# Attention by heads in small tiles, and the splitting's middle word in PSUM

## The chip, the cores and the metric

The kernel runs on one core of a Trainium2 chip, as one program. The metric is the device time of an execution in microseconds (us), lower is better. The core has five engines with queues of their own: TensorE (PE; its weight loads are shown apart as PEld), VectorE (DVE), ScalarE (ACT), GpSimd (POOL) and SyncE (SP, which issues most transfers). Each engine works through its own queue in the order in which the program wrote it.

## The reference

Three layers follow one another, all in float32 (two weight matrices come in float64):

```python
kv = einsum('bhsd,bhse->bhde', k, v)            # 8 batches, 8 heads, 576 tokens, 64 wide
out = einsum('bhsd,bhde->bhse', q, kv)
x = out / sqrt(mean(out*out, -1) + 1e-6) * g_norm      # per head; then 4608 tokens x 512
h = x @ w_in                                    # 512 -> 2048, float64 weights
x = (maximum(h, 0) + alpha * minimum(h, 0)) @ w_out    # 2048 -> 512
logits = x @ w_gate + modality_bias[modality_id]       # 8 experts, the best one per token
out = gate * (maximum(x @ w1[e], 0) @ w2[e])    # 512 -> 1024 -> 512, each token by its expert
```

## The kernel before

The 4608 tokens go through attention and the dense layer in 12 chunks of 384 tokens, each three tiles of 128. A chunk has 16 steps, one per block of 128 of the 2048 hidden columns. In step s, `first(c, s)` makes the hidden block from `xhi` and `xlo` (x split in two for precision), 12 matmuls that move 384 columns. DVE makes `gg` from it (the bent line with alpha), ACT rounds it to `ghi`, POOL makes the rest `glo`, and one step later `second(c, s - 1)` adds to the three outputs with 9 matmuls that move 512 columns. After the twelve chunks the tokens, scattered by expert into DRAM, are gathered in tiles of 128 and go through their experts (`layer1`, `layer2`).

What the next chunk needs is woven into the steps of the present one. `load_kv` and `kv_mm` bring in a new batch's k and v (seven of the twelve chunks have one) and multiply them, in one pair of heads per step, steps 2 to 5; the last block of 64 rows is a matmul of its own height. `kv_evict` (step 6) writes the two 64 x 64 products of each pair onto the diagonal of `kvbd`, whose other corners stay zero. `attend` (steps 9, 10, 11, one tile each) multiplies q with that block diagonal, four pairs of heads with 128 x 128 weights each. Where a tile lies in two batches, its halves are matmuls of their own, with 64 columns of weights. ACT copies the result to `x` and squares it, DVE sums the squares (`squares`), takes the root in thirteen small steps (`rsqrt`, step 12) and scales (`scale_x`, steps 13 and 14). At step 15 `turn_x` turns x with twelve PE transposes through PSUM, and `take_x` makes `xhi` (ACT) and `xlo` (DVE) from PSUM with the norm's factor `g_sb`.

The router of the chunk before is woven in too: DVE's `dots` (steps 1 to 8), `choose` (step 8: the one-hot `hb`), `count` (two small PE matmuls on `hb`) and `weigh` (step 9), `place` (step 10) and three indirect scatters on POOL (steps 10 to 12). Except in four steps, a piece of the experts' weights is split and stored ahead (`pre_load`, `pre_hi`, `pre_lo`, `pre_store`).

Chunk 0 also splits the float64 weights, 32 halves of 128 x 512, two or more per step (`cut`). Of the two words of a float64 number ACT takes the high one (`cut_a`), and DVE makes a middle word in three instructions: `low_bits` (L163), `sign_bit` (L168), and `high_bits` (L173), which shifts the high word and joins it with the middle one. `cut_c` rounds on ACT (L181) and subtracts on POOL (L182). The middle word `cut_b` lives in SBUF, in two buffers of the later `wg_sb`.

PSUM has eight banks: three for the outputs of `second`, two for `first`, three for all else (`other`). The order of all work is written out by hand (`manual_schedule`); the program's order on each engine is the order of execution.

Of the kernel before, what the change touches and what calls it, by code (L numbers as in the profile page):

```python
# [11 lines left out]
I32 = mybir.dt.int32  # L12
# [32 lines left out]
def fused(ctx: ExitStack, tc, qT, kv, g2, wmoe, alpha, wgate, bias, modality, w12, out):  # L45
# [14 lines left out]
    ps_h = phase1.enter_context(tc.tile_pool(name="ps_h", bufs=2, space=PSUM))  # L60
    ps_a = phase1.enter_context(tc.tile_pool(name="ps_a", bufs=3, space=PSUM))
    pools = []
# [7 lines left out]
    nalpha = one.tile([128, NFB], F32, name="nalpha")  # L70
    g_sb = one.tile([128, 1], F32, name="g_sb")
    pad = one.tile([128, ROW], F32, name="pad")
# [8 lines left out]
    base = one.tile([128, E], F32, name="base")  # L81
    kvbd = [one.tile([128, 4, 128], F32, name=f"kvbd{i}") for i in range(2)]
    xhi = one.tile([128, 4, CT], F32R, name="xhi")
    xlo = one.tile([128, 4, CT], F32R, name="xlo")
# [10 lines left out]
    lg_t, kvps, hot_t, tps_t, pos_t, sq_t, rsqrt_t, yb_t = {}, {}, {}, {}, {}, {}, {}, {}  # L95
    ops = []

# [16 lines left out]
    def load_kv(b, p):  # L114
        if b == 0 and p >= 2:
            o = (p - 2) * 1280
            t = scratch[:, o:o + 1280].rearrange("p (s c) -> p s c", c=256)
        else:
            t = two.tile([128, 5, 256], F32, tag="kv", name="kv")
# [37 lines left out]
    def cut_b(n):  # L157
        o = 3072 + (n % 2) * 512
        return scratch[:, o:o + 512].bitcast(I32)

    def low_bits(n):
        if n < 2 * NFB:
            V.tensor_scalar(cut_b(n).unsqueeze(2), raw_t[n][:, :, 0:1].bitcast(U32), 2.0 ** -29, 7.0, ALU.mult, ALU.min)  # L163
# [20 lines left out]
    def cut(later=None, between=None):  # L184
        h = n_cut[0]
        n_cut[0] += 1
        cut_c(h)
        steps = [lambda: sign_bit(h + 1), lambda: low_bits(h + 2), lambda: high_bits(h + 1)]
        if later is None:
            for step in steps:  # L190
                step()
        else:
            later.extend(steps)
        if between:
            between()
        cut_a(h + 2)
        load_w(h + 7)
# [21 lines left out]
    def kv_mm(b, p):  # L219
        if p == 0:  # L220
            kvps[b] = four(other())
        t = kv_t.pop((b, p))
        for s in range(5):
            n = 128 if s < 4 else 64
            PE.matmul(kvps[b][:, p, :], t[0:n, s, 0:128], t[0:n, s, 128:256], start=(s == 0), stop=(s == 4))

# [4 lines left out]

    def attend(c, t):
        bank4 = other()
        ps = four(bank4)
        tok = c * CT + t * 128
        b0, b1 = tok // S, (tok + 127) // S
        q = q_t[c]
        for p in range(4):
            if b0 == b1:
                PE.matmul(ps[:, p, :], q[:, p, t * 128:(t + 1) * 128], kvbd[b0 % 2][:, p, :], start=True, stop=True)  # L240
            else:
                for i, b in enumerate((b0, b1)):
                    o = t * 128 + i * 64
                    PE.matmul(ps[i * 64:i * 64 + 64, p, :], q[:, p, o:o + 64], kvbd[b % 2][:, p, :], start=True, stop=True)
        x = three.tile([128, 8, 64], F32, tag="x", name="x")
        xt_t[c, t] = x
        flat = bank4
        A.copy(x.rearrange("p a b -> p (a b)"), flat)
        A.activation(junk, flat, AF.Square)

# [62 lines left out]
    def scale_x(c, t):  # L313
        x = xt_t[c, t]
        src = ops[t].rearrange("p a (h b) -> p (a h) b", b=64) if c == 0 and t < 2 else x
        r = ms_t[c][:, t * 8:t * 8 + 8].unsqueeze(2).to_broadcast([128, 8, 64])
        (G if c == 0 and t == 2 else V).tensor_tensor(x, src, r, ALU.mult)

    def turn_x(c, k):
        if k == 3:  # L320
            ps = bank(CT)
        else:
            ps = other(CT)
        for t in range(3):
            x = xt_t[c, t].rearrange("p a b -> p (a b)")
            PE.transpose(ps[:, t * 128:(t + 1) * 128], x[:, k * 128:(k + 1) * 128], ident)
        tps_t[k] = ps

    def take_x(k):
        ps = tps_t.pop(k)  # L330
        A.activation(xhi[:, k, :], ps, AF.Identity, scale=g_sb)
        V.scalar_tensor_tensor(xlo[:, k, :], ps, g_sb, xhi[:, k, :].bitcast(F32), ALU.mult, ALU.subtract)  # L332

# [98 lines left out]
    def count(c):  # L432
        hot, hb, lg = hot_t[c]
        ps = other(48).rearrange("p (n a b) -> p n a b", n=2, a=3)
# [142 lines left out]
    def load_rows(i):  # L577
# [5 lines left out]
        r = G.value_load(tab, min_val=0, max_val=E * BUCKET + 1024 - 128)  # L583
        rows[i] = three.tile([128, 4, 128], F32, tag="x", name="rows")
        src = xb[ds(r, 128)]
# [81 lines left out]
    def turn_h(i):  # L667
        h = hh.pop(i)
        hi = two.tile([128, 2, 512], F32R, tag="kv", name="hth")
        lo = two.tile([128, 2, 512], F32R, tag="raw", name="htl", bufs=3)  # L670
# [63 lines left out]
    with tc.manual_schedule():  # L734
# [13 lines left out]
        for i in range(2):  # L748
            V.memset(kvbd[i], 0.0)
        V.memset(magic, 0x5F3759DF)  # L750


# [7 lines left out]
        warm(WARM[0])  # L760
        ops.extend(four(other()) for _ in range(3))
        ms_t[0] = one.tile([128, 24], F32, tag="ms", name="ms")
        for t in range(3):
            xt_t[0, t] = three.tile([128, 8, 64], F32, tag="x", name="x")
        for p in range(5):
# [16 lines left out]
        for t in range(3):  # L782
            sum_half(t, 1)
        A.copy(xt_t[0, 2].rearrange("p a b -> p (a b)"), ops[2].rearrange("p a b -> p (a b)"))
        for n in range(3, 6):
# [10 lines left out]
        for k in range(4):  # L796
            turn_x(0, k)
            take_x(k)
        high_bits(1)
        V.tensor_scalar(nalpha, alpha_sb, -1.0, None, ALU.mult)  # L800
        cut_a(2)
        low_bits(2)
        load_w(6)
# [7 lines left out]
        for c in range(NCH):  # L811
# [3 lines left out]
            for s in range(NFB):  # L815
                edge = s == NFB - 1
                if edge and nxt < NCH:
                    for k in range(2):
                        turn_x(nxt, k)
                between = None  # L820
                if edge and nxt < NCH:
                    between = lambda: [take_x(k) for k in range(2)]
                elif s == 0 and c > 0:
                    between = lambda: [second(c - 1, NFB - 1, (2,)), y_out(c - 1, 1)]
# [16 lines left out]
                if edge and nxt < NCH:  # L841
                    for k in range(2, 4):
                        turn_x(nxt, k)
                        take_x(k)
                    second(c, s, (0, 1))
                elif edge:
                    turn_rows(0)
                    second(c, s)

                if kvb and s < 4:  # L850
                    load_kv(kvb[0], s)
                if kvb and 2 <= s < 6:
                    kv_mm(kvb[0], s - 2)
                if kvb and s == 6:
                    kv_evict(kvb[0])
                if nxt < NCH:
# [3 lines left out]
                    if at <= s < at + 3:  # L860
                        attend(nxt, s - at)
                    if s == 11 and nxt + 1 < NCH:
# [5 lines left out]
                    if s == 13:  # L868
                        scale_x(nxt, 0)
                        scale_x(nxt, 1)  # L870
                    if s == 14:
                        scale_x(nxt, 2)

                if c > 0:
# [13 lines left out]
                    if nxt < NCH and 10 <= s < 13:  # L888
                        scatter(c - 1, [s - 10])
                    if nxt == NCH and s == 10:  # L890
# [27 lines left out]
        pools.append(ctx.enter_context(tc.tile_pool(name="ps_p", bufs=2, space=PSUM)))  # L918
        pools.append(ctx.enter_context(tc.tile_pool(name="ps_o", bufs=1, space=PSUM)))

        add = lambda *js: [far_add(c, j) for j in js]
# [95 lines left out]
```

## Time and profile before

| | us |
|---|---|
| median of 3 runs | 1484.96 (1483.78 to 1485.65) |
| profiled execution | 1483.74 |
| its span | 1482.1 |
| PE busy | 1410.6 (95%) |
| PE weight loads busy | 1207.5 (81%) |
| DVE busy | 1077.2 (73%) |
| POOL busy | 704.3 (48%) |
| ACT busy | 526.0 (35%) |

The span runs from the first to the last instruction. Matmuls are pipelined: a matmul's duration is its way through the array, and the next one starts before it ends. What one costs is read from start to start. An fp32 matmul shows as two passes, a split one (fp32r) as one. The mean granted clock of PE is 0.989 of 2.4 GHz.

### The profile page before, as it was taken

The numbers are of one execution on the slowest core, as the hardware profiler recorded it, in microseconds if no ns is written. First come the engines' busy times: TensorE is split into PE (matmuls) and PEld (weight loads), VectorE is DVE, ScalarE is ACT, GpSimd is POOL, SyncE is SP. The second block draws the span as 40 slices with busy tenths as digits, with TensorE's granted clock in tenths as the row PEclk, the third lists the DMA queues.
The fourth block names the chain that finished last, engine by engine and source line by source line (L and its number), as shares of the span: only waits on it lengthen the run. The fifth ranks groups of instructions, "written<-read, shape, count | busy, mean of one in ns | idle before, by whom it ended". The sixth has DMA issues, their size and how long they took to land. (4 is left out here: it accounts for less than half of the span.)

```text
span 1482.1 us, 22781 instructions
## 1 busy us (share of the span) xinstructions
PE 1410.6 (95%) x6914; PEld 1207.5 (81%) x6914; DVE 1077.2 (73%) x2210; ACT 526.0 (35%) x1075; POOL 704.3 (48%) x706
## 2 busy tenths in 40 slices
PE   8887999999999999999999999888999999999997
PEld 7666888888988888898888888676888888888886
DVE  6997977677876867787777687929666666666664
ACT  3563222322232222222222323204444544544543
POOL 2664645455655545564545464556433333333321
PEclk9999999999999999999999999999999999999999
DMA  8643445454445454355454353353732144447784
GB/s 280 216 160 121 171 147 195 144 197 150 149 166 176 149 192 145 133 171 190 142 181 163 126 172 106 129 199 148 258 101 58 44 166 155 155 156 276 271 308 192
DMA packets 80966, 250.45 MB, mean 169 GB/s; under 512 B 12429, under 2 KB 30861, under 8 KB 78672
## 3 DMA queue, kind: packets, MB, share of 16 engines
q1 hardware_dynamic: 68128, 219.25, 42.1%
q0 software_dynamic: 12720, 29.72, 6.6%
q8 instruction: 63, 1.03, 0.3%
q14 instruction: 55, 0.45, 0.1%
HBM read 158.69 MB, written 91.54 MB: 169 GB/s over the span
## 5 line engine op out<-in xcount | busy, mean ns | idle before, releaser
L342 PE MATMUL h<-xhi,W 128*128 128x384 f32 x1536 | 436.3, 345 | 1.7 <-POOL W L182 1.3
L356 POOL TENSOR_TENSOR glo<-gg,ghi 128x384 fp32r<-128x384 f32 x192 | 234.1, 1220 | 416.1 <-ACT ghi L354 389.3
L370 PE MATMUL y<-W,ghi 128*128 128x512 f32 x1152 | 308.3, 403 | 28.6 <-ACT ghi L354 24.8
L342 PEld LDWEIGHTS h<-xhi,W 128*128 128x128 f32 x1536 | 285.0, 190 | 13.1 <-POOL W L182 2.0
L389 DVE CUSTOM_DVE_ANT_0 junk<-yrow,wg_sb 128x512 f32<-128x512 f32 x278 | 283.2, 1019 | 6.7
L370 PEld LDWEIGHTS y<-W,ghi 128*128 128x128 f32 x1152 | 213.2, 190 | 74.0 <-ACT ghi L354 33.5
L342 PE MATMUL h<-xlo,W 128*128 128x384 f32 x768 | 261.2, 341 | 0.0
L354 ACT CAST ghi<-gg 128x384 fp32r<-128x384 f32 x192 | 98.6, 514 | 379.8 <-DVE gg L350 241.5
L349 DVE TENSOR_SCALAR gg<-h,alpha_sb 128x384 f32<-128x384 f32 x176 | 107.9, 613 | 165.8 <-PE h L342 164.3
L624 PE MATMUL y<-W,hth 128*128 (+1 forms) x656 | 207.0, 397 | 1.3 <-ACT hth L680 1.3
L624 PE MATMUL h<-W,xhi 128*128 (+1 forms) x656 | 206.9, 397 | 0.0
L212 POOL TENSOR_TENSOR raw<-raw 128x512 f32<-128x512 f32 x128 | 202.3, 1581 | 0.2
L370 PE MATMUL y<-W,glo 128*128 128x512 f32 x576 | 168.5, 401 | 6.8 <-POOL glo L356 6.8
L700 POOL DMA_INDIRECT out_dram<-kvbd,tail x41 | 42.5, 1036 | 267.2 <-ACT kvbd L698 259.9
L208 ACT CAST raw<-raw 128x512 fp32r<-128x512 f32 x128 | 79.5, 621 | 213.7 <-DMA raw<-in_w_dram 197.6
L342 PEld LDWEIGHTS h<-xlo,W 128*128 128x128 f32 x768 | 146.0, 190 | 5.4 <-DVE xlo L332 0.2
L624 PEld LDWEIGHTS y<-W,hth 128*128 128x128 f32 x656 | 123.3, 188 | 31.4 <-ACT hth L680 1.7
L624 PEld LDWEIGHTS h<-W,xhi 128*128 128x128 f32 x656 | 123.9, 189 | 29.3
L370 PEld LDWEIGHTS y<-W,glo 128*128 128x128 f32 x576 | 107.9, 191 | 36.7 <-POOL glo L356 12.2
L624 PE MATMUL h<-W,xlo 128*128 (+1 forms) x328 | 130.2, 397 | 2.3 <-DVE xlo L613 2.3
L660 DVE TENSOR_SCALAR hh<-h 32x256 f32<-32x256 f32 x304 | 126.7, 417 | 6.3 <-PE h L624 1.7
L681 DVE TENSOR_TENSOR htl<-hh,hth 128x512 fp32r<-128x512 f32 x76 | 52.6, 692 | 108.2 <-ACT hth L680 108.2
(188 smaller groups left out, 1676.4 us busy)
## 6 DMA issues: line engine op xcount, KB each, us to landing
wsp<-raw SPq DMA_DIRECT2D x128, 512.0 KB, 2.9
W<-wsp SPq DMA_DIRECT2D x16, 4096.0 KB, 13.5
raw<-in_w_dram SPq DMA_DIRECT2D x128, 256.0 KB, 3.3
kv<-in_kv_dram SPq DMA_DIRECT2D x30, 512.0 KB, 4.6
rows<-xb POOLq DMA_DIRECT2D x164, 64.0 KB, 2.5
raw<-in_wmoe_dram SPq DMA_DIRECT2D x17, 512.0 KB, 3.3
qT<-in_qT_dram SPq DMA_DIRECT2D x11, 768.0 KB, 5.3
wg_sb<-in_wmoe_dram SPq DMA_DIRECT2D x15, 512.0 KB, 3.4
```

What stands on the lines that cost most here:

```text
L208: A.copy(sp_t[n][:, 0:512].bitcast(F32R), sp_t[n][:, 512:1024])
L212: G.tensor_tensor(lo, lo, hi, ALU.subtract)
L342: PE.matmul(ps, w_at(fb, part)[:, k * 128:(k + 1) * 128], x[:, k, :], start=(i == 0), stop=(i == 11))
L349: V.tensor_scalar(gg, ps, 0.0, alpha_sb[:, fb:fb + 1], ALU.min, ALU.mult)
L354: A.copy(ghi, gg)
L356: G.tensor_tensor(glo, gg, ghi.bitcast(F32), ALU.subtract)
L370: PE.matmul(y_t[c][t], a[:, t * 128:(t + 1) * 128], w, start=(fb == i == 0), stop=(fb == NFB - 1 and i == 2))
L389: V.tensor_tensor_reduce(junk, yb_t[c][t][:, 0:D], wg_sb[:, e, :], 1.0, 0.0, ALU.mult, ALU.add, lg_t[c][:, t, e:e + 1])
L624: m = PE.matmul(ps, a, w, start=start, stop=stop)
L660: m = V.tensor_scalar(to, of, 0.0, None, ALU.max) if mine else A.activation(to, of, AF.Relu)
L681: V.tensor_tensor(v, x, u.bitcast(F32), ALU.subtract)
L700: d = G.indirect_dma_start(out=out, out_offset=IndirectOffsetOnAxis(ap=tail[:, i, 1:2].bitcast(I32), axis=0), in_=y, in_offset=None, bound ...
```

## The change

- `kv_mm` makes only the two 64 x 64 products that are used, on two halves of the array's columns, over five blocks of 128 rows; the fifth block's lower half is zeroed once, in k and v buffers of their own (`kvt`). Two pairs go together, in steps 3 and 6, and their loads in steps 0 and 3.
- `attend` works by heads: for every 32 tokens, pair and head of the pair, a matmul with 64 rows and 32 columns of weights (q) that moves the 64 columns of that head's product. The token's place within its 32 and the pair are the partition of the result. Tiles 0 and 1 go in step 9, tile 2 in step 11; `attended` copies and squares by head.
- x is turned by DVE in 32 x 32 blocks in place (`turn_x`, steps 13 and 14), and `take_x` reads SBUF. w_in and g_norm are permuted to fit. The first chunk, which has its own prologue, still uses PE transposes (`turn_first`).
- `other` has two banks instead of three. The third, `spare`, holds the third tile of the first attention, then the middle word of the splitting (one buffer; `low_bits` of a half now comes after `high_bits` of the half before), and from chunk 1 on the counts.
- `count`, `place` and the scatters are one step later, except in the last chunk.
- x and the experts' gathered rows live in `xs`, and the experts' `hth` in a pool of its own.

```diff
-    ps_a = phase1.enter_context(tc.tile_pool(name="ps_a", bufs=3, space=PSUM))
+    ps_a = phase1.enter_context(tc.tile_pool(name="ps_a", bufs=2, space=PSUM))
+    spare = phase1.enter_context(tc.tile_pool(name="ps_s", bufs=1, space=PSUM)).tile([128, 512], F32, name="spare")
+    kvt = phase1.enter_context(tc.tile_pool(name="kvp", bufs=1)).tile([128, 2, 5, 256], F32, name="kvt")
...
     def cut_b(n):
-        o = 3072 + (n % 2) * 512
-        return scratch[:, o:o + 512].bitcast(I32)
+
+        return (scratch[:, 3072:3584] if n < 2 else spare).bitcast(I32)
...
-        steps = [lambda: sign_bit(h + 1), lambda: low_bits(h + 2), lambda: high_bits(h + 1)]
+        steps = [lambda: low_bits(h + 1), lambda: sign_bit(h + 1), lambda: high_bits(h + 1)]
...
         for s in range(5):
-            n = 128 if s < 4 else 64
-            PE.matmul(kvps[b][:, p, :], t[0:n, s, 0:128], t[0:n, s, 128:256], start=(s == 0), stop=(s == 4))
+            for o in (0, 64):
+                PE.matmul(kvps[b][o:o + 64, p, o:o + 64], t[:, s, o:o + 64], t[:, s, 128 + o:192 + o], start=(s == 0), stop=(s == 4))
...
+    def attend(c, ts):
+
         q = q_t[c]
...
+        ps = [other(256 * len(ts)).rearrange("p (a b) -> p a b", b=64) for _ in range(2)]
+        for a in range(4 * len(ts)):
+            o = ts[0] * 128 + 32 * a
+            kvs = kvbd[(c * CT + o) // S % 2]
+            for p in range(4):
+                for h in range(2):
+                    r = slice(64 * h, 64 * h + 64)
+                    PE.matmul(ps[h][32 * p:32 * p + 32, a, :], q[r, p, o:o + 32], kvs[r, p, r], start=True, stop=True)
+        for i, t in enumerate(ts):
+            ops_t[c, t] = [p[:, 4 * i:4 * i + 4, :] for p in ps]
+
+    def attended(c, t):
+        ps = ops_t.pop((c, t))
+        x = xs[:, t, :].rearrange("p (a h b) -> p a h b", a=4, h=2)
+        sq = junk.rearrange("p (a h b) -> p a h b", a=4, h=2)
+        xt_t[c, t] = xs[:, t, :].rearrange("p (a b) -> p a b", b=64)
+        for h in range(2):
+            A.copy(x[:, :, h, :], ps[h])
+            A.activation(sq[:, :, h, :], ps[h], AF.Square)
...
+        src = ops[t] if t < 2 else last
+        to = xs[:, t, :].rearrange("p (h e a i) -> p a h e i", h=2, e=2, a=4)
+        for h in range(2):
+            (G if t == 2 else V).tensor_tensor(
...
+    def turn_x(c, t):
+        x = xs[:, t, :]
+        V.transpose(x, x)
+
+    def take_x(c, k):
+        if c:
+            of = xs.rearrange("p t (a k j) -> p (t a) k j", a=4, k=4)[:, :, k]
         else:
...
+            of = turn_first(k).rearrange("p (a j) -> p a j", j=32)
+        hi, lo = (x[:, k, :].rearrange("p (a j) -> p a j", j=32) for x in (xhi, xlo))
+        A.activation(hi, of, AF.Identity, scale=g_sb[:, k:k + 1])
+        V.scalar_tensor_tensor(lo, of, g_sb[:, k:k + 1], hi.bitcast(F32), ALU.mult, ALU.subtract)
...
-                if kvb and s < 4:
-                    load_kv(kvb[0], s)
-                if kvb and 2 <= s < 6:
-                    kv_mm(kvb[0], s - 2)
+                if kvb and s in (3, 6):
+                    kv_mm(kvb[0], s - 3 and 2)
+                    kv_mm(kvb[0], (s - 3 and 2) + 1)
+                if kvb and s in (0, 3):
+                    load_kv(kvb[0], s and 2)
+                    load_kv(kvb[0], (s and 2) + 1)
...
+                        if s != at + 1:
+                            attend(nxt, (0, 1) if s == at else (2,))
+                        attended(nxt, s - at)
...
+                    late = nxt < NCH
                     if s == 24 // per + 1:
+                        weigh(c - 1)
+                    if s == 24 // per + 1 + late:
                         count(c - 1)
-                        weigh(c - 1)
-                    if s == 24 // per + 2:
+                    if s == 24 // per + 2 + late:
                         place(c - 1)
```

## Rows read from the trace of the kernel before

**Rows 1.** Stretches (chunk 0; chunks 1 to 10): us, then busy us by engine, clock, DMA.
```profile
22.90:137.80 114.90, 89.39 (x418) 72.75 (x419) 106.38 (x136) 62.08 (x123) 69.57 (x50) 0.94 0.48 166
137.80:914.50 776.70, 759.75 (x4006) 676.75 (x4005) 591.17 (x1290) 218.31 (x416) 417.43 (x357) 1.00 0.48 162
```
**Rows 2.** Groups by line, DVE in chunk 0: count | busy us, mean ns | idle before.
```profile
L173 DVE SCALAR_TENSOR_TENSOR wa<-wa,wg_sb 128x512 int32<-128x512 int32 x31 | 31.7, 1023 | 2.6 <-ACT wa L154 2.6
L168 DVE SCALAR_TENSOR_TENSOR wg_sb<-raw,wg_sb 128x512 int32<-128x512 int32 x15 | 16.6, 1106 | 0.1
...
L163 DVE TENSOR_SCALAR wg_sb<-wg_sb 128x512 int32<-128x512 uint32 x15 | 12.8, 851 | 0.0
```
**Rows 3.** Single lines on DVE: duration in ns min/median/max, first and last start.
```profile
L163 DVE TENSOR_SCALAR wg_sb<-raw x17: 410/418/1509, 14.9 to 119.6; 128x512 int32<-128x512 uint32 x17
...
L350 DVE SCALAR_TENSOR_TENSOR gg<-h,gg x176: 556/557/560, 140.8 to 998.8; 128x384 f32<-128x384 f32 x176
...
L616 DVE STREAM_TRANSPOSE rows<-rows x38: 704/705/712, 1039.8 to 1449.3; 128x512 f32<-128x512 f32 x38
```
**Rows 4.** PE's waits in chunks 1 to 10: us in total, times, longest.
```profile
PE a L326 <- DVE x L317: 6.2, 10, 0.6
PE a L435 <- DVE hb L416: 5.8, 8, 0.8
```
**Rows 5.** Timeline of PE, step 2 of chunk 2 (kv products): start, us, instructions.
```profile
223.34 1.47 PE L225 MATMUL a<-kv 128*128 128x128 f32 x10
224.74 0.44 PE L342 MATMUL h<-xhi,W 128*128 128x384 f32 x1
225.02 0.34 PE L342 MATMUL h<-xlo,W 128*128 128x384 f32 x1
```
**Rows 6.** Timeline of PE, attention in chunk 0, in one batch and across two.
```profile
89.64 0.86 PE L370 MATMUL y<-W,glo 128*128 128x512 f32 x3
90.34 1.05 PE L240 MATMUL a<-kvbd,qT 128*128 128x128 f32 x8
...
91.40 0.34 PE L342 MATMUL h<-xlo,W 128*128 128x384 f32 x1
91.58 0.34 PE L342 MATMUL h<-xhi,W 128*128 128x384 f32 x1
...
96.26 0.86 PE L370 MATMUL y<-W,glo 128*128 128x512 f32 x3
97.05 1.09 PE L244 MATMUL a<-kvbd,qT 128*64 128x128 f32 x16
...
98.36 0.34 PE L342 MATMUL h<-xlo,W 128*128 128x384 f32 x1
```
**Rows 7.** Timeline of PE, the end of chunk 2 (transposes at the edge).
```profile
288.11 1.57 PE L370 MATMUL y<-W,ghi 128*128 128x512 f32 x6
289.51 0.87 PE L370 MATMUL y<-W,glo 128*128 128x512 f32 x3
290.22 0.49 PE L326 MATMUL a<-ident,x 128*128 128x128 f32 x3
...
290.80 1.63 PE L370 MATMUL y<-W,ghi 128*128 128x512 f32 x6
```
**Rows 8.** Register instructions of PE's sequencer, three stretches: ns min/median/max, first and last start.
```profile
L633 PEldq ALU_OP  x1: 36/36/36, 1082.5 to 1082.5; - x1
...
L636 PEldq FUSED_REGOPS  x1: 138/138/138, 1082.8 to 1082.8; - x1
...
L624 PEldq FUSED_REGOPS  x8: 46/46/46, 1051.6 to 1052.5; - x8
```
**Rows 9.** Timeline of DVE in chunk 2, steps 6 and 15.
```profile
246.50 0.43 DVE L230 COPY kvbd<-a 64x256 f32<-64x256 f32 x1 [0.93 <-ACT kvbd L229]
...
288.38 0.62 DVE L349 TENSOR_SCALAR gg<-h,alpha_sb 128x384 f32<-128x384 f32 x1 [2.93 <-PE h L342]
```
**Rows 10.** Timeline of PE, step 14 of chunk 0.
```profile
128.08 0.30 PE L326 MATMUL a<-ident,x 128*128 128x128 f32 x1 [2.85 <-DVE x L317]
```

More of the change, by code (lines that the diff above doesn't have):

```diff
@@ L70, in fused @@
     nalpha = one.tile([128, NFB], F32, name="nalpha")
-    g_sb = one.tile([128, 1], F32, name="g_sb")
+    g_sb = one.tile([128, 4], F32, name="g_sb")
     pad = one.tile([128, ROW], F32, name="pad")
@@ L82, in fused @@
     kvbd = [one.tile([128, 4, 128], F32, name=f"kvbd{i}") for i in range(2)]
+    xs = one.tile([128, 3, D], F32, name="xs")
     xhi = one.tile([128, 4, CT], F32R, name="xhi")
@@ L95, in fused @@
     lg_t, kvps, hot_t, tps_t, pos_t, sq_t, rsqrt_t, yb_t = {}, {}, {}, {}, {}, {}, {}, {}
-    ops = []
+    ops, ops_t = [], {}
     def bank(n):
@@ L118, in load_kv @@
         else:
-            t = two.tile([128, 5, 256], F32, tag="kv", name="kv")
+            t = kvt[:, p % 2]
         SP.dma_start(t[:, 0:4, :], kv[b, p, 0:512].rearrange("(t p) c -> p t c", p=128))
@@ L230, in kv_evict @@
         V.tensor_copy(kvbd[b % 2][64:128, :, 64:128], ps[64:128, :, 64:128])
[L232 to L236, printed above, removed]
-        q = q_t[c]
[L238 to L249, printed above, removed]
+    def attend(c, ts):
+        q = q_t[c]
+        ps = [other(256 * len(ts)).rearrange("p (a b) -> p a b", b=64) for _ in range(2)]
[16 more added lines that the diff above has]
+            A.activation(sq[:, :, h, :], ps[h], AF.Square)
     def kv_pair(p):
@@ L313, in scale_x, with turn_first @@
     def scale_x(c, t):
[L314 to L321, printed above, removed]
-        else:
[L323 to L332, printed above, removed]
+        r = ms_t[c][:, t * 8:t * 8 + 8]
+        if c:
+            x = xt_t[c, t]
+            V.tensor_tensor(x, x, r.unsqueeze(2).to_broadcast([128, 8, 64]), ALU.mult)
+            return
+        src = ops[t] if t < 2 else last
+        to = xs[:, t, :].rearrange("p (h e a i) -> p a h e i", h=2, e=2, a=4)
+        for h in range(2):
+            (G if t == 2 else V).tensor_tensor(
+                to[:, :, h], src.rearrange("p a (h e i) -> p a h e i", h=2, e=2)[:, :, h],
+                r.rearrange("p (a h) -> p a h", h=2)[:, :, h:h + 1].unsqueeze(3).to_broadcast([128, 4, 2, 32]), ALU.mult)
+    def turn_first(k):
+        ps = (other, other, lambda n: spare[:, 0:n], bank)[k](CT)
+        for t in range(3):
+            PE.transpose(ps[:, t * 128:(t + 1) * 128], xs[:, t, k * 128:(k + 1) * 128], ident)
+        return ps
+    def turn_x(c, t):
+        x = xs[:, t, :]
+        V.transpose(x, x)
+    def take_x(c, k):
+        if c:
+            of = xs.rearrange("p t (a k j) -> p (t a) k j", a=4, k=4)[:, :, k]
+        else:
+            of = turn_first(k).rearrange("p (a j) -> p a j", j=32)
+        hi, lo = (x[:, k, :].rearrange("p (a j) -> p a j", j=32) for x in (xhi, xlo))
+        A.activation(hi, of, AF.Identity, scale=g_sb[:, k:k + 1])
+        V.scalar_tensor_tensor(lo, of, g_sb[:, k:k + 1], hi.bitcast(F32), ALU.mult, ALU.subtract)
     def first(c, fb, between=None):
@@ L433, in count @@
         hot, hb, lg = hot_t[c]
-        ps = other(48).rearrange("p (n a b) -> p n a b", n=2, a=3)
+        ps = (other(48) if pools else spare[:, 0:48]).rearrange("p (n a b) -> p n a b", n=2, a=3)
         PE.matmul(ps[:, 0].rearrange("p a b -> p (a b)"), tri, hb.rearrange("p a b -> p (a b)"), start=True, stop=True)
@@ L583, in load_rows @@
         r = G.value_load(tab, min_val=0, max_val=E * BUCKET + 1024 - 128)
-        rows[i] = three.tile([128, 4, 128], F32, tag="x", name="rows")
+        rows[i] = four(xs[:, i % 3, :])
         src = xb[ds(r, 128)]
@@ L668, in turn_h @@
         h = hh.pop(i)
-        hi = two.tile([128, 2, 512], F32R, tag="kv", name="hth")
+        hi = pools[2].tile([128, 2, 512], F32R, tag="kv", name="hth")
         lo = two.tile([128, 2, 512], F32R, tag="raw", name="htl", bufs=3)
@@ L750, in fused @@
         V.memset(magic, 0x5F3759DF)
+        V.memset(kvt[64:128, :, 4, :], 0.0)
         def warm(n):
@@ L760, in fused @@
         warm(WARM[0])
-        ops.extend(four(other()) for _ in range(3))
+        ops.extend(four(b) for b in (other(), other(), spare))
         ms_t[0] = one.tile([128, 24], F32, tag="ms", name="ms")
-        for t in range(3):
-            xt_t[0, t] = three.tile([128, 8, 64], F32, tag="x", name="x")
         for p in range(5):
@@ L783, in fused @@
             sum_half(t, 1)
-        A.copy(xt_t[0, 2].rearrange("p a b -> p (a b)"), ops[2].rearrange("p a b -> p (a b)"))
+        last = three.tile([128, ROW], F32, tag="yrow", name="last")[:, 0:D].rearrange("p (a b) -> p a b", b=128)
+        A.copy(last, ops[2])
         for n in range(3, 6):
@@ L796, in fused @@
         for k in range(4):
-            turn_x(0, k)
-            take_x(k)
+            take_x(0, k)
         high_bits(1)
@@ L801, in fused @@
         cut_a(2)
-        low_bits(2)
         load_w(6)
@@ L816, in fused @@
                 edge = s == NFB - 1
-                if edge and nxt < NCH:
-                    for k in range(2):
-                        turn_x(nxt, k)
                 between = None
                 if edge and nxt < NCH:
-                    between = lambda: [take_x(k) for k in range(2)]
+                    between = lambda: [take_x(nxt, k) for k in range(2)]
                 elif s == 0 and c > 0:
@@ L842, in fused @@
                     for k in range(2, 4):
-                        turn_x(nxt, k)
-                        take_x(k)
+                        take_x(nxt, k)
                     second(c, s, (0, 1))
@@ L860, in fused @@
                     if at <= s < at + 3:
-                        attend(nxt, s - at)
+                        if s != at + 1:
+                            attend(nxt, (0, 1) if s == at else (2,))
+                        attended(nxt, s - at)
                     if s == 11 and nxt + 1 < NCH:
@@ L870, in fused @@
                         scale_x(nxt, 1)
+                        turn_x(nxt, 0)
                     if s == 14:
                         scale_x(nxt, 2)
+                        turn_x(nxt, 1)
+                        turn_x(nxt, 2)
                 if c > 0:
@@ L887, in fused @@
                             scatter(c - 1, range(3))
-                    if nxt < NCH and 10 <= s < 13:
-                        scatter(c - 1, [s - 10])
+                    if nxt < NCH and 11 <= s < 14:
+                        scatter(c - 1, [s - 11])
                     if nxt == NCH and s == 10:
@@ L919, in fused @@
         pools.append(ctx.enter_context(tc.tile_pool(name="ps_o", bufs=1, space=PSUM)))
+        pools.append(ctx.enter_context(tc.tile_pool(name="hts", bufs=2)))
         add = lambda *js: [far_add(c, j) for j in js]
@@ L989 @@
     w_in, w_out = inputs["moe_w_in"], inputs["moe_w_out"]
-    a_in = w_in.reshape(4, 128, NFB, 128).transpose(2, 1, 0, 3).reshape(NFB, 128, 512)
+    a_in = w_in.reshape(4, 4, 32, NFB, 128).transpose(3, 0, 2, 1, 4).reshape(NFB, 128, 512)
+    g4 = np.tile(inputs["g_norm"].reshape(1, 2, 32).transpose(0, 2, 1), (4, 1, 2)).reshape(128, 4)
     w1, w2 = inputs["moe2_w1"], inputs["moe2_w2"]
@@ L997 @@
         "kv": np.concatenate([pairs(k), pairs(v)], axis=3),
-        "g2": np.concatenate([inputs["g_norm"], inputs["g_norm"]]).reshape(128, 1),
+        "g2": g4,
         "wmoe": np.stack([a_in, w_out.reshape(NFB, 128, 512)], axis=1).view(np.int64),
```

## The prediction

> **What bounds the kernel now.** I began with the table of stretches [rows 1], which splits the span by stage. In chunks 1 to 10 PE is busy 759.75 of 776.70 us: PE is the bound, and what leaves its queue there shortens the kernel. In chunk 0 (114.90 us) PE is busy for only 89.39 and DVE for 106.38, so DVE bounds it. The last chunk and the experts keep their instructions. The groups of DVE instructions in chunk 0 [rows 2] then say what fills DVE: the three instructions that cut the float64 words. Their durations one by one [rows 3] show why: low_bits takes 0.41 or 1.5 us, with a median of 0.418, so it has two speeds, while the gg instruction that reads one operand from PSUM never leaves 0.556 to 0.560. PE's waits [rows 4], short timelines of PE [rows 5 to 7], the register instructions of PE's sequencer [rows 8] and two timelines [rows 9, 10] price the rest.
>
> **kv products.** Before, a pair of heads is five fp32 matmuls, each shown as two passes: 10 passes in 24.74 - 23.34 = 1.40 us, and the next matmul starts its second step 0.28 us later instead of 0.175, so 1.50 [rows 5]. A batch is four pairs, 6.0 us. After, two pairs stand together, as 20 matmuls on two column halves. Of such halves the trace has one example, attention across two batches [rows 6]: 16 passes start in pairs, eight steps in all, and from 97.05 to the second step of the next matmul pass 1.31 us, against 1.06 for eight full passes. Entry is 0.79 against 0.70. So halves cost the same step (0.11 us for two passes of 128 columns) and 0.25 + 0.09 = 0.34 to go in and out. The new passes move 64 columns instead of 128. The step is then between 0.11 (no gain) and half of it; I take 0.055, since 384 columns step in 0.18 and 512 in 0.23 [rows 6, 7], so steps follow columns. A group: 20 passes a half x 0.055 + 0.34 = 1.44, a batch 2.88, saved 3.1. Six batches fall in chunks 1 to 10: -18.7.
>
> **Attention.** Before, a chunk has 24 passes x 0.11 = 2.66 us. After, it has 96 matmuls of 64 rows x 32 columns that move 64 columns, in two groups, over eight places of the array. If all eight run at once, as the two halves do, it is 24 steps x 0.055 = 1.3. But 96 instructions must also be handed out. The nearest rows are PE's register instructions among the expert matmuls [rows 8]: eight of them, one matmul behind each, start within 0.9 us, 0.124 apart (0.9 / 7, rounded), and without matmuls they start 0.1 apart (1082.5 to 1082.8 in three). A matmul costs 0.024 if the 0.1 is the register instruction's, and 0.078 if only its own 0.046 is. An fp32 matmul has two passes, so perhaps twice the lower. I take 0.036: 3.46 + 2 x 0.34 = 4.14, 1.48 more per chunk. Ten chunks +14.8, less 1.0 for the three in which attention across batches paid its own 0.34: +13.8.
>
> **Transposes and the edge.** Twelve transposes a chunk leave PE: six (two rows of three, of which the first stands) take 290.80 - 290.22 = 0.6 us and the next matmul steps a little late, 0.11 each [rows 7], so 1.3. Their waits for the scaled x go too, 6.2 in ten chunks [rows 4]. Together -19.4. DVE gets three 32x32 transposes of 0.705 [rows 3], 2.1 us, in steps 13 and 14. It idled 2.93 us before the gg of step 15 [rows 9]; PE now comes there 0.65 + 0.62 earlier, so 2.93 - 2.1 - 1.27 is 0.4 short. xlo, queued behind that gg, now reads two SBUF operands and may meet POOL. second(15), which waits for ghi, has 0.2 of slack: I give back 0.3 a chunk, +3.0 (bounds 0 and +15). On ACT, copy and square become four half-size instructions; ACT is busy 218 of 777 us [rows 1], and this costs nothing. Were ACT late, weigh behind it would be, and through DVE the gg of step 10.
>
> **Counts one step later.** PE no longer waits for the one-hot: -5.8 [rows 4]. place and scatter shift by one step with it, past one precut on POOL, nothing in front of PE; were POOL late, glo would be by one precut. kv_evict now waits for products of its own step. Behind it on DVE are the dots and then the next gg, which second waits for. DVE waits 0.93 there today [rows 9]; it will wait until about 3.5 us after first(6), but PE is then 1.4 longer in that step, so the lag stays. I return +1.0 of the 5.8. load_kv goes out in twos, the second two behind a wait for the products of step 3; behind them on SP are that step's precut store and load, with three buffers: nothing, or at most 1 us a batch.
>
> Chunks 1 to 10: -18.7 + 13.8 - 19.4 + 3.0 - 5.8 + 1.0 = -26.1.
>
> **Chunk 0.** The cut takes 31.7 us of L173, 32.5 of L168 (two like groups) and 25.5 of L163 (two), 89.7 in 91 instructions [rows 2]. With the middle word in PSUM each has at most one SBUF tensor. The row for that is gg: 0.557 for 384 columns without spread [rows 3]; 128 columns more make 0.69 (L163 then loses its 0.41, which is in the sum). 91 x 0.69 = 62.8, so -26.9; the new transposes +2.1. DVE's other 8.5 us of idle I leave: 114.9 - 24.8 = 90.1. Of that, 5 us are the edge, where PE waits up to 2.85 us for x [rows 10] and will not; then 85. On the other side, POOL with 69.6 us and ACT with 62 work in turns with DVE, and a chunk that gains only 10 is the bound. The order low, sign, high with one buffer adds no wait across engines: all three are DVE's, in order. PE here is cover, not bound.
>
> **The rest.** In the prologue the scaling is cut in two, four instructions of 256 columns at about 0.43 [rows 9] for two of about 0.69: +0.3. Buffers that change place (rows, kv, the experts' hi) keep their number: 0.
>
> **Sum.** The profiled execution took 1483.74 us. -26.1 - 24.8 + 0.3 = -50.6: 1433. The median of the runs shown is 0.08% above that execution, so about 1434.
>
> **Rivals.** (1) Slower: a small matmul costs what it costs in the one example of halves, 8 matmuls in eight steps of 0.11, so 0.11 each, because starts and not columns set the step. Attention is then 96 x 0.11 + 0.68 = 11.2 a chunk and the kv group 2.5: + 11 x 7.1 + 14 x 1.1 = +93, 1527. It decides from 0.078 per matmul: (0.078 - 0.036) x 1056 + (0.078 - 0.055) x 280 = 51. For it: each matmul has its own load of weights. Against it: the two halves start almost together and then wait out the step, so columns fill it. Chance 0.12. (2) The hand-out binds: 0.05 to 0.078 per matmul, at the middle of 0.064 + 1056 x 0.028 + 280 x 0.009 = +32, 1466; at the top no change. For it: the upper reading of rows 8. Chance 0.20. The Trainium skill, "TensorE: Matmul & The Clock Gate", section "Wait — 56ns, not 53.3ns?", speaks for this one: without hardware decode the sequencer spends about 62 ns per MATMUL, which binds once the array's work is shorter; by that figure the sum would be 1464, as an estimate from that page, and no run here shows which decode is in use. (3) Chunk 0 is held by the turns between ACT, DVE and POOL and gives 10: 1449. For it: POOL's subtractions follow ACT's copies one by one; against it: DVE at 106 of 115. Chance 0.12.
>
> **How the numbers follow.** Forecast 0.56, rivals 0.12, 0.20 and 0.12. The lower end: attention at 1.3 a chunk (-22) and chunk 0 at 85 (-5) give 1406, with rounding 1403. The upper end takes in (3) and most of (2): 1475. Within 0.2% (3 us) is about what a measurement of this kernel can't tell from no change. (2) lends 0.04 to that and 0.01 to slower, with 0.01 of the others beside it. Faster 0.82, same 0.05, slower 0.13.
>
> **What would show it.** Right: kv groups of about 1.4 us, attention of the first two tiles about 2.3 us, no wait of PE for x or the one-hot, the three cutting instructions at 0.69 without a second speed, chunk 0 at about 90. Wrong: attention groups over 5 us (rivals 1, 2); a second speed of the cutting instructions in PSUM; DVE's lag at steps 9 to 15 turning into waits of PE for ghi of over 1 us a chunk; a granted clock of 1.2 GHz (0.5) in stretches with small matmuls.

## The result, and the profile after

The changed kernel takes 1441.67 us (median of four runs, 1440.3 to 1442.34) against 1485.02 for the kernel before on the same chip: ratio 0.971, 95% interval 0.969 to 0.973. Its profiled execution took 1442.01 us with a span of 1440.4. The forecast was 1434, 8 us too low.

The stretches of the kernel after, in the columns of [rows 1]: prologue, chunk 0, chunks 1 to 10, chunk 11, experts.

```profile
0.00:23.20 23.20, 20.39 (x146) 18.36 (x146) 11.80 (x41) 5.94 (x13) 2.33 (x9) 1.00 0.93 321
23.20:114.30 91.10, 79.46 (x606) 64.92 (x607) 85.28 (x139) 62.02 (x129) 57.64 (x49) 0.98 0.62 208
114.30:875.70 761.40, 736.35 (x5781) 647.03 (x5780) 618.82 (x1320) 220.60 (x476) 407.02 (x358) 0.99 0.49 166
875.70:963.90 88.20, 75.16 (x346) 65.05 (x345) 52.60 (x117) 14.86 (x29) 46.79 (x46) 0.94 0.47 164
963.90:1440.40 476.50, 462.89 (x2003) 374.68 (x2001) 316.43 (x634) 224.61 (x496) 167.82 (x247) 0.99 0.48 176
```

Against the kernel before the prologue is 0.3 longer, chunk 0 is 23.8 shorter (114.90 to 91.10; forecast 24.8), chunks 1 to 10 are 15.3 shorter (776.70 to 761.40; forecast 26.1), chunk 11 is 0.1 longer and the experts are 3.0 shorter (479.5 to 476.5; forecast 0). In chunks 1 to 10 PE now stands idle for 25.05 of 761.40 us, where it stood idle for 16.95 of 776.70. So its busy time shrank by 23.4, and 8.1 of that was lost to waits.

A step runs from the first matmul of one `first` to that of the next. By steps, chunks 1 to 10 changed as follows, in us over all ten chunks:

| steps | what is in them | before | after | change |
|---|---|---|---|---|
| 0 | `first` alone | 28.11 | 35.15 | +7.04 |
| 1 to 8 | key-value products | 373.70 | 356.92 | -16.78 |
| 9 to 12 | attention, counts | 204.84 | 196.28 | -8.56 |
| 14, 15 | the edge (the next chunk's x is scaled, turned and taken) | 127.89 | 130.95 | +3.06 |

Step 13 takes 42.13 in both.

DVE's groups in chunk 0 (count, busy us, mean ns, idle before), which answer to [rows 2]:

```profile
L176 DVE SCALAR_TENSOR_TENSOR wa<-wa,spare 128x512 int32<-128x512 int32 x30 | 20.6, 687 | 2.9
...
L171 DVE SCALAR_TENSOR_TENSOR spare<-raw,spare 128x512 int32<-128x512 int32 x15 | 10.4, 696 | 0.5
...
L166 DVE TENSOR_SCALAR spare<-wg_sb 128x512 int32<-128x512 uint32 x15 | 10.3, 690 | 0.2
```

The three lines of the cut, at 1023, 1106 and 851 ns before, all take 0.69. One line by itself (min/median/max):

```profile
L166 DVE TENSOR_SCALAR spare<-raw x15: 678/687/698, 26.0 to 102.5; 128x512 int32<-128x512 uint32 x15
```

The two speeds of [rows 3] (410 to 1509 ns) are gone. PE's waits in chunks 1 to 10, which answer to [rows 4]:

```profile
PE y L389 <- ACT ghi L373: 25.0, 21, 2.0
```

The waits for x and for the one-hot are gone. The wait for ghi, 4.9 us in all and at most 0.5 before, is now 25.0 and up to 2.0: 20.0 of it stands in step 15, at the edge. PE there in chunk 2, then DVE, then POOL:

```profile
259.99 0.86 PE L389 MATMUL y<-W,glo 128*128 128x512 f32 x3
262.84 1.66 PE L389 MATMUL y<-W,ghi 128*128 128x512 f32 x6 [1.99 <-ACT ghi L373]
```

```profile
256.36 3.52 DVE L324 TENSOR_TENSOR xs<-xs,it 128x512 f32<-128x512 f32 x1
259.81 1.29 DVE L342 STREAM_TRANSPOSE xs<-xs 128x512 f32<-128x512 f32 x2
261.03 0.57 DVE L368 TENSOR_SCALAR gg<-h,alpha_sb 128x384 f32<-128x384 f32 x1
```

```profile
256.03 1.00 POOL L474 DMA_INDIRECT xb<-yrow,pos  x1 [0.28 <-POOL pos L473]
257.05 1.31 POOL L215 TENSOR_TENSOR raw<-raw 128x512 f32<-128x512 f32 x1
258.30 1.02 POOL L375 TENSOR_TENSOR glo<-gg,ghi 128x384 fp32r<-128x384 f32 x1
```

Read them from below. POOL works from 256.03 to 259.32 without a gap: a scatter, a precut (`pre_lo`, the subtraction that splits a piece of the experts' weights), glo. DVE's third scaling of x (L324, both operands in SBUF) starts behind the scatter's start and ends only after glo, 3.52 us instead of 0.68. The transposes and the gg of step 15 queue behind it, so ghi and `second(15)` are late. After the stall the granted clock falls in six of the ten chunks: step 0 takes 3.54 to 4.33 us there and 2.81 in the other four. Chunk 5, PE, and below it the stretch with its granted clock (the number before the last two):

```profile
414.05 2.10 PE L389 MATMUL y<-W,ghi 128*128 128x512 f32 x6 [1.99 <-ACT ghi L373]
415.95 0.52 PE L361 MATMUL h<-xhi,W 128*128 128x384 f32 x1
416.27 0.52 PE L361 MATMUL h<-xlo,W 128*128 128x384 f32 x1
```

```profile
415.95:419.35 3.40, 3.40 (x14) 3.40 (x13) 0.32 (x1) 0.00 (x0) 0.00 (x0) 0.63 0.33 104
```

The matmuls step by 0.32 instead of 0.175, the lower of the clock's two levels (1.2 GHz) for most of these 3.4 us. That is the +7.04 of step 0, where nothing was changed.

### The profile page after: what moved, and what is told of

It reads as the page before. It is cut to its first block, busy times and chain, and to the rows that moved or that the text cites. A ratio compares the mean times of both kernels' runs of the same rounds, so it can differ in the third digit from the quotient of the medians.

```text
span 1440.4 us, 26864 instructions
## 1 busy us (share of the span) xinstructions
PE 1374.2 (95%) x8878; PEld 1170.0 (81%) x8878; DVE 1084.9 (75%) x2246; ACT 528.0 (37%) x1141; POOL 681.6 (47%) x707
## 5 line engine op out<-in xcount | busy, mean ns | idle before, releaser
L375 POOL TENSOR_TENSOR glo<-gg,ghi 128x384 fp32r<-128x384 f32 x192 | 227.3, 1184 | 399.3 <-ACT ghi L373 374.1
L361 PEld LDWEIGHTS h<-xhi,W 128*128 128x128 f32 x1536 | 289.3, 193 | 12.8 <-ACT xhi L350 1.4
L408 DVE CUSTOM_DVE_ANT_0 junk<-yrow,wg_sb 128x512 f32<-128x512 f32 x278 | 270.8, 974 | 6.7
L643 PE MATMUL y<-W,hth 128*128 (+1 forms) x656 | 203.9, 392 | 1.3 <-ACT hth L699 1.3
L215 POOL TENSOR_TENSOR raw<-raw 128x512 f32<-128x512 f32 x128 | 197.2, 1541 | 0.5
```

What stands on the lines that cost most here:

```text
L215: G.tensor_tensor(lo, lo, hi, ALU.subtract)
L361: PE.matmul(ps, w_at(fb, part)[:, k * 128:(k + 1) * 128], x[:, k, :], start=(i == 0), stop=(i == 11))
L375: G.tensor_tensor(glo, gg, ghi.bitcast(F32), ALU.subtract)
L408: V.tensor_tensor_reduce(junk, yb_t[c][t][:, 0:D], wg_sb[:, e, :], 1.0, 0.0, ALU.mult, ALU.add, lg_t[c][:, t, e:e + 1])
L643: m = PE.matmul(ps, a, w, start=start, stop=stop)
```

## The experiments

Theory: POOL's unbroken work at step 13 holds the third scaling, and the stall and the clock follow. Rival: the three transposes that DVE gained are too much for it, wherever POOL's work stands. Two runs break POOL's row in different ways. The first puts counts and scatters back one step:

```diff
-                    late = nxt < NCH
+                    late = False
...
-                    if nxt < NCH and 11 <= s < 14:
-                        scatter(c - 1, [s - 11])
+                    if nxt < NCH and 10 <= s < 13:
+                        scatter(c - 1, [s - 10])
```

> Undoes one part of the change: count, place and the scatters one step earlier again (steps 9, 10 and 10 to 12). Theory A: PE's wait for ghi at the end of every chunk (2.0 us, 25 us in ten chunks with that of step 13) comes from POOL: the scatter that moved into step 13 stands ahead of the precut there and of glo, and DVE's third scaling (3.52 us instead of 0.68 to 1.64) waits until POOL is through. Then the scaling falls to about 1.6 us, the wait at the edge to under 0.5 us, the clock stays at 2.4 GHz over the chunk starts, and the time is about 1442 - 18 - 7 = 1417 us; the wait for the one-hot doesn't come back, because attention in step 9 is now 0.6 us longer. Theory B: the wait is the price of DVE's three transposes (2.1 us); then the edge stays at 12.9 us in steps 14 and 15 and the time is 1442 us, or up to 1448 us if the wait for the one-hot comes back.

Measured: 1410.65 us (1408.47 to 1411.88), ratio 0.950 (0.948 to 0.951), 31 faster than the change and 6 faster than the theory's sum. This version is called early counts below. Chunks 1 to 10:

```profile
114.00:845.20 731.20, 724.89 (x5781) 639.41 (x5780) 594.86 (x1320) 220.97 (x476) 407.97 (x358) 1.00 0.52 172
```

and DVE's third scaling and POOL in chunk 2:

```profile
254.01 1.05 DVE L324 TENSOR_TENSOR xs<-xs,it 128x512 f32<-128x512 f32 x1
254.99 1.29 DVE L342 STREAM_TRANSPOSE xs<-xs 128x512 f32<-128x512 f32 x2
```

```profile
253.22 1.30 POOL L215 TENSOR_TENSOR raw<-raw 128x512 f32<-128x512 f32 x1
254.80 1.14 POOL L375 TENSOR_TENSOR glo<-gg,ghi 128x384 fp32r<-128x384 f32 x1 [0.28 <-ACT ghi L373]
```

Here the scaling takes 1.05, ends 0.54 after the precut, and runs beside the first part of glo. Steps 14 and 15 last 5.02 and 5.75 (12.79 a chunk before, 13.10 after the change, 10.77 here), step 0 is 2.81 again, and the clock stays at 1.00. PE's wait for the one-hot does not come back either, although the counts are where they were before the change. The second run leaves the counts late and moves the precut out of step 13:

```diff
-                    if s not in (10, 11, 14, 15):
+                    if s not in (11, 13, 14, 15):
```

> Keeps the counts late, and moves the precut of step 13 (load, split, store) to step 10. Theory A (POOL holds DVE's third scaling): POOL's run of scatter, precut and glo in steps 13 and 14 gets 1.3 us shorter, the scaling takes about 2.2 us instead of 3.52, the wait for ghi at the edge falls from 2.0 to about 0.7 us: 1442 - 13 and most of the clock loss, 1423 to 1430 us. Theory B (DVE's transposes): no change at the edge, 1442 us.

Measured: 1411.5 us (1409.47 to 1413.28), ratio 0.950 (0.949 to 0.952), where 1423 to 1430 had been expected. The scatter still stands beside the scaling, which is no longer held (min/median/max of all 33):

```profile
L324 DVE TENSOR_TENSOR xs<-xs,it x33: 681/683/693, 106.9 to 840.3; 128x512 f32<-128x512 f32 x33
```

So the scatter alone holds nothing, and the transposes, which both runs keep, cost PE nothing that shows. It is the scatter and the precut in one step, with glo behind them. The rival falls.

How this row of three holds the scaling so long is not shown. That POOL leaves no gap is not enough. In chunk 2 of the kernel before, DVE and then POOL were:

```profile
283.81 1.64 DVE L317 TENSOR_TENSOR x<-x,it 128x512 f32<-128x512 f32 x1
```

```profile
283.61 1.29 POOL L212 TENSOR_TENSOR raw<-raw 128x512 f32<-128x512 f32 x1
284.86 1.45 POOL L356 TENSOR_TENSOR glo<-gg,ghi 128x384 fp32r<-128x384 f32 x1
```

Precut and glo stand without a gap there too, yet the scaling ended at 285.45, 0.55 after the precut and before glo's end at 286.31. After the change it ended 0.55 after glo. It was also held from the scatter on: 0.68 after its start at 256.36 it would have been through before the precut began at 257.05. Why the scatter, harmless alone, makes that difference stays open.

**Chunk 0.** The middle word goes back to SBUF, with two buffers and the old order:

```diff
     def cut_b(n):
...
-        return (scratch[:, 3072:3584] if n < 2 else spare).bitcast(I32)
+        o = 3072 + (n % 2) * 512
+        return scratch[:, o:o + 512].bitcast(I32)
...
-        steps = [lambda: low_bits(h + 1), lambda: sign_bit(h + 1), lambda: high_bits(h + 1)]
+        steps = [lambda: sign_bit(h + 1), lambda: low_bits(h + 2), lambda: high_bits(h + 1)]
...
+        low_bits(2)
```

> Undoes one part: the middle word of the splitting goes back to two SBUF buffers, with the old order of the three cutting instructions. If the two-speed instructions on DVE made chunk 0 slow, chunk 0 goes back from 91 to about 112 to 115 us and the time is 1463 to 1466 us. If chunk 0's gain came from the kv products, the attention and the edge without PE transposes (those waits were 3.9 us, and 5 us of DVE idle), chunk 0 gives back under 12 us: below 1454 us.

Measured: 1464.34 us (1461.97 to 1467.91), ratio 0.986 (0.984 to 0.988); chunk 0 takes 111.57 instead of 91.10, and the mean of the group goes back towards its old 1023 ns:

```profile
L176 DVE SCALAR_TENSOR_TENSOR wa<-wa,wg_sb 128x512 int32<-128x512 int32 x31 | 29.5, 952 | 2.6 <-ACT wa L157 2.6
```

The PSUM operand (with its order, which was not tried apart from it) is worth 20.5 of the 23.8. POOL pays for the SBUF word as well: it is busy for 69.83 us in chunk 0 here, 57.64 with the word in PSUM, and its subtraction of the cut (L185) has a mean of 1652 ns here and 1302 there.

**Size of the groups.** Attention in three groups of one tile, first on the change itself:

```diff
-                        if s != at + 1:
-                            attend(nxt, (0, 1) if s == at else (2,))
+                        attend(nxt, (s - at,))
```

> One size: attention in three groups of one tile (steps 9, 10, 11) instead of two groups of two and one. If what a group costs beside its matmuls is the change of array tiling (step 9 is 1.51 us over a plain step for 64 matmuls, step 11 0.98 for 32: 0.45 us per group and 0.017 us per matmul), eleven chunks pay 0.45 us more each: +5, 1447 us. If the hand-out of matmuls sets the time and the fixed part is only the fill of the array's queue, the third group costs under 0.15 us: 1442 to 1443 us.

1448.24 us (1446.45 to 1449.38), ratio 0.975 (0.974 to 0.977). The total agrees with the theory, but steps 9 to 11 grew by only 2.5 us over ten chunks (153.1 to 155.6), and steps 14, 15 and 0, with the stall and the clock, by 3.1. So this run decides nothing, and the same edit was made again on early counts, which has no stall. This run and those after it were taken on other chips than early counts; the kernel before took 1484.19 and 1483.92 us there and 1484.95 beside early counts, so they compare to about 1 us.

> Base is the version with the counts placed early (1410.65 us). Attention goes in three groups of one tile instead of two and one. Theory A (a group costs 0.45 us to go in and out beside its matmuls): one group more in 11 chunks, +5, about 1415.6 us. Rival B (a group costs half of that or less, as the steps of the earlier run with three groups say, 15.53 against 15.31 for the three steps): +2.4 or less, 1411 to 1413 us.

1416.75 us (1413.53 to 1419.19), ratio 0.954 (0.952 to 0.956). Steps 9 to 11 take 15.54 against 15.19, and chunks 1 to 10 735.10 against 731.20: 0.35 to 0.39 a group, nearer to the theory's 0.45 than to the rival's half of it.

**Key-value products.** One 128 x 128 matmul per block again, in the new groups, also on early counts:

```diff
-            for o in (0, 64):
-                PE.matmul(kvps[b][o:o + 64, p, o:o + 64], t[:, s, o:o + 64], t[:, s, 128 + o:192 + o], start=(s == 0), stop=(s == 4))
+            PE.matmul(kvps[b][:, p, :], t[:, s, 0:128], t[:, s, 128:256], start=(s == 0), stop=(s == 4))
```

> Base is the version with the counts placed early (1410.65 us). The only edit: a key-value product is one 128x128 matmul per block again, in groups of two pairs, instead of two 64-column halves. Theory A (the halves pay because they move half the columns): 20 passes x 0.11 + entry and exit against 1.52 a group, so about +0.75 for each of 14 groups, +10.5, about 1421 us, and the step with a group goes from 5.62 to about 6.4 us. Rival B (the gain came only from leaving the half-empty last block and from fewer groups): the same, 1409 to 1413, the step stays at 5.6.

1418.78 us (1416.34 to 1419.25), ratio 0.955 (0.954 to 0.957). The group after, and the group here, each with the matmul behind it:

```profile
203.62 1.39 PE L228 MATMUL a<-kvt 128*64 128x64 f32 x40
204.93 0.44 PE L361 MATMUL h<-xhi,W 128*128 128x384 f32 x1
```

```profile
217.51 2.39 PE L227 MATMUL a<-kvt 128*128 128x128 f32 x20
219.66 0.42 PE L360 MATMUL h<-xhi,W 128*128 128x384 f32 x1
```

1.31 against 2.15 from start to start; the step is 6.36 instead of 5.62, +0.74 where +0.75 was expected. The total grew by 8.1 and not by 10.5, because waits in step 6 went away: over the six batches of chunks 1 to 10 its length beyond the group's own came to 2.4 with early counts and to 0.3 here. Twice the passes with half the columns, on two halves of the array, are the cheaper form. The theory holds.

**A small matmul.** Each attention matmul issued twice, on early counts:

```diff
-                for h in range(2):
+                for h in (0, 1, 0, 1):
```

> Base is the version with the counts placed early (1410.65 us). Each attention matmul is issued twice (the second writes the same result). Theory A, from the traces after: 0.017 us a matmul, 96 x 11 chunks = 1056 of them, +18, about 1429 us; the step with two tiles grows by 1.1, the one with one tile by 0.55. Rival B, the figure of the prediction, 0.036 a matmul: +38, about 1449 us. Rival C, 0.11 a matmul: +116, about 1527 us.

1471.82 us (1467.31 to 1471.87), ratio 0.992 (0.990 to 0.993): 61 more, which none of the three expected. The group of two tiles, without the doubling (early counts) and with it:

```profile
229.70 1.48 PE L245 MATMUL a<-kvbd,qT 64*32 64x64 f32 x128
231.12 0.19 PE L454 MATMUL spare<-hb,tri 128*128 128x24 bf16 x1
```

```profile
236.96 2.39 PE L245 MATMUL a<-kvbd,qT 64*32 64x64 f32 x188
242.02 1.03 PE L245 MATMUL a<-kvbd,qT 64*32 64x64 f32 x68 [2.66 <-issue]
242.98 0.19 PE L454 MATMUL spare<-hb,tri 128*128 128x24 bf16 x1
243.04 0.42 PE L361 MATMUL h<-xhi,W 128*128 128x384 f32 x1
```

188 passes (94 matmuls) go at 0.0127 a pass, then PE stands for 2.66 us and waits for nothing that the profile shows ("issue"), and the rest follows. PE's waits over the whole kernel:

```profile
PE a L245 <- issue: 22.6, 9, 3.6
```

Without such a stop the added 64 matmuls cost 1.75 in step 9 (7.54 against 5.79, chunks 8 and 10) and 32 cost 0.95 in step 11 (6.05 against 5.10): 0.027 to 0.030 each. 1056 of them make about 30, the stops 22.6, and the lower clock behind some stops adds to it: in three chunks step 10 has a granted clock of 0.68 to 0.72 and is 1.4 to 1.8 longer. The profiled execution, the fastest of the four, is 55.7 above that of early counts. A group of 64 matmuls, as the change has it, shows no such stop in chunks 1 to 10. I take it that PE starts a group with matmuls already handed out while longer work ran, and that this stock ends somewhere above 64. That is argued and not shown: no run here measures such a stock by itself, and in chunks 8 and 10 the doubled group of step 9 went through without a stop.

**The experts.** Their hi buffers start at another place in SBUF after the change. On early counts a gap of 32 bytes gives them the same offset as before (32 modulo 64):

```diff
         pools.append(ctx.enter_context(tc.tile_pool(name="hts", bufs=2)))
+        pools[2].tile([128, 8], F32, tag="gap", name="gap", bufs=1)
```

> Base is the version with the counts placed early (1410.65 us), whose expert stage takes 476.6 us. The experts' two hi buffers are shifted by 32 bytes, so that their start is 32 modulo 64 as in the kernel before, instead of 0; nothing else changes. Theory A (the place of these buffers in SBUF set the 3 us that the experts gained): the expert stage goes back to about 479.5 and the time to about 1413.6 us, the mean of the matmuls on hth from 392 to 397 ns. Rival B (not this alignment): no change, 476.6 and 1410.7 us.

1415.12 us (1413.14 to 1416.2), ratio 0.953 (0.952 to 0.955). The matmuls on hth with early counts, and with the gap (count, busy us, mean ns, idle):

```profile
L643 PE MATMUL y<-W,hth 128*128 (+1 forms) x656 | 204.0, 392 | 1.3 <-ACT hth L699 1.3
```

```profile
L643 PE MATMUL y<-W,hth 128*128 (+1 forms) x656 | 207.0, 396 | 1.3 <-ACT hth L699 1.3
```

That is the 207.0 of the kernel before, while the change and its seven variants above all have 203.9 or 204.0; the expert stage takes 480.3 instead of 476.6. So the place of these two buffers is the cause. ghi, glo and the experts' lo buffers also lay at 32 modulo 64, so a gap of 32 bytes ahead of them was the next step:

```diff
+    two.tile([128, 8], F32, tag="gap", name="gap", bufs=1)
...
```

Further gaps of 32 bytes keep the key-value buffer and hth at 0 modulo 64, so hth lies 64 bytes further on. In the second of these runs the first gap stands among the buffers ahead of q instead.

> Base is the version with the counts placed early (1410.65 us). Only places in SBUF change: ghi, glo, gg and the experts' lo buffers start at 0 modulo 64 bytes instead of 32; the experts' hi buffers and the key-value buffer stay at 0. Theory A, from the run that shifted the hi buffers (matmuls on them 5 ns slower at 32): the step of the matmuls on ghi and glo goes from 234 to 229 ns, 144 of them in each of 11 chunks that PE bounds, 7.9 us, and 328 in the experts, 1.6 us: about 1401 us. Rival B (the 5 ns belong to the experts' loop alone): the lo buffers only, or nothing, 1409 to 1411 us.

> As the run with ghi, glo and the lo buffers at 0 modulo 64, and with q and the experts' hh at 0 too. Theory A (a matmul's stationary operand is what counts, and q is one, in 96 small matmuls a chunk that are not held by it): within 2 us of that run, about 1400. Rival B (small matmuls gain 5 ns each as well): 5 us less, 96 x 11 x 0.005, about 1396.

1413.08 us (1410.79 to 1416.88), ratio 0.952 (0.951 to 0.954), and 1412.63 (1411.72 to 1414.03), ratio 0.952 (0.951 to 0.953): no gain. In both the mean on ghi fell to 397 ns from the 401 of early counts. That on glo, 399 with early counts and up to 402 in other runs that leave its place alone, did not fall (401 and 403), that on the lo buffers went from 397 to 399, and that on hth rose too, although hth kept its offset of 0. In the first of them:

```profile
L646 PE MATMUL y<-W,hth 128*128 (+1 forms) x656 | 205.6, 395 | 1.3 <-ACT hth L702 1.3
```

So the offset by itself is not the rule. What in a buffer's place counts stays open.

## Why the prediction was right, and where not

The total is within 8 us by luck: two large errors cancel. By its steps:

- **Chunk 0**, -24.8: measured -23.8. Of the cut's 91 instructions, 90 take 62.0 us (20.6 + 2 x 10.4 + 10.3 + 10.3) and the last 0.7, where 62.8 was worked out, and putting the word back undoes 20.5 of the gain. Right in mechanism and size; rival 3 is out, and POOL's 69.6, which spoke for it, fell to 57.6 with the word in PSUM.
- **Key-value products**, -18.7, with the 1.0 returned for `kv_evict` -17.7: measured -16.8 in steps 1 to 8. The group costs 1.41 in its own step and 0.11 in the next, 1.52 instead of 1.44. Right: steps follow columns. The second group's step is 1.3 longer than that over six batches: in the longest (chunk 6, 6.29 us) ACT first casts a piece of the experts' weights whose transfer came late, and PE waits 0.40 for the ghi behind it.
- **Attention and counts**, +13.8 - 5.8 = +8.0: measured -8.6 in steps 9 to 12. Mis-sized: the term "I take 0.036" per matmul. Taking the two groups' added time in steps 9 and 11 as one price per matmul and one per group, 1.51 = 64 m + g and 0.98 = 32 m + g, gives m = 0.017 and g = 0.45 (0.35 to 0.39 by the third group). A chunk is 2.5 to 2.8 instead of 4.14 and costs about what it cost before. The 0.036 came from the pace at which PE's sequencer hands out register instructions and matmuls among the experts [rows 8]. It was a choice between bounds that another stage gave, and a short group behind long matmuls does not pay that pace. Rivals 1 and 2 are out for this kernel; the stops in groups twice as long may be what the second feared. The Trainium skill's 62 ns per MATMUL ("TensorE: Matmul & The Clock Gate", "Wait — 56ns, not 53.3ns?") is not what these groups show: 64 matmuls in 1.51 us, all included, are 0.024 each.
- **The edge**, -19.4 + 3.0 = -16.4: measured +3.1 in steps 14 and 15, and +7.0 in step 0 behind it. This step failed, and not in the -19.4: without the stall (early counts) the two steps give 10.77 against 12.79 a chunk, -20.2 in ten. What failed is "I give back 0.3 a chunk (bounds 0 and +15)" together with "place and scatter shift by one step with it, past one precut on POOL, nothing in front of PE". I looked for POOL's harm in POOL's own queue and at xlo. It came earlier on DVE, at the third scaling, held for 3.52 us and ahead of the gg on which `second(15)` rests. The kernel before had a sign of it that I did not use: its third scaling took 1.64 instead of 0.68 in each of chunks 1 to 10, beside the same precut. A second sign stood under "what would show it wrong" (waits for ghi of over 1 us a chunk: 2.5 were measured, 0.5 of them as before); its price, 29.5 with the clock where 3.0 had been given back, lay outside the bounds.
- **Counts later**, inside the terms above: the waits for the one-hot did go, but they stay away with early counts too. So the lateness gained nothing and cost about 31 us through the scatter's new neighbour.
- **Prologue** +0.3: measured +0.3, which confirms nothing: kernels with this same prologue took from 22.6 to 24.5 us for it. **Experts** 0: measured -3.0; a buffer that keeps its number but changes its place was not free of effect.

The sum: edge with step 0 +26.5 against its forecast, attention and counts -16.6, key-value with `kv_evict` +0.9, chunk 0 +1.0, experts -3.0, the rest about 0: +8.8 of the 8.9 by which the profiled executions missed (-41.7 against -50.6).

The version with early counts beats both kernels, 1410.65 us; moving one precut instead gives the same.

## What to carry to other kernels

When a step of one engine's queue is moved, look at which instructions of the *other* engines it will now stand beside, not only at its own queue: here moving a scatter by one step put it beside a precut, and the two, with glo behind them, held a DVE instruction with two SBUF operands for 3 us. Give such a DVE instruction one operand in PSUM where a bank is free (in chunk 0 that helped POOL too), and keep long rows of POOL's work away from it where none is. A total close to the forecast says little about the terms: compare step by step, since an error of +26 and one of -17 stood behind 8 us here.

## What the runs showed that was not expected

- A DVE instruction with both operands in SBUF was held across a scatter, a precut and glo on POOL (3.52 us instead of 0.68); with a precut and glo alone, back to back, it took 1.64 and ended before glo did. The Trainium skill ("SBUF — State Buffer", "Who interferes with whom") calls the ports that DVE shares with GpSimd an exclusive lock. The 1.64, which ended 0.55 after the precut, agrees; the 3.52 went on past the precut's end and through glo. The same section has a DVE instruction with at most one SBUF input outside its two-port modes free of POOL, and the 0.69 of the cut with its word in PSUM agrees.
- A PE stall of 2 us was followed by a lower granted clock in six of ten chunks (0.63 over 3.4 us in chunk 5), so a stall cost up to 1.5 us more in step 0 than itself (4.33 instead of 2.81).
- A burst of 256 small passes stopped on its way in eight of ten chunks: in the timeline above it ran at 0.0127 us a pass and stopped after 188, for 2.66 us.
- 32 bytes in the place of two SBUF buffers changed the mean of the matmuls that read them by 4 ns, 3 to 4 us in this kernel.
